# Fourier partial sums through DRAM and a later transposing transfer, in a kernel that weaves attention into an FNet product

## The chip, the cores and the metric

The kernel runs on one core of one Trainium2 chip. The metric is the device time of one execution in microseconds; the core has five engines with a queue each (PE for matrix products, DVE, ACT, POOL, and SP, which here issues every DMA) that are ordered against each other by semaphores alone.

## The reference

Two independent parts, whose results stand side by side in the output (2048 x 1152, f32).

```python
# part A: x [1, 2048, 576], 32 heads of 18, N = 4 segments of L = 512
q, k, v = (x @ wq, x @ wk, x @ wv)          # split in heads and segments
for s in range(4):
    logits = qs @ ks.T * 18 ** -0.5 + mask  # mask: -1e9 where key index > query index
                                            # ar[:, None] < ar[None, :]
    a_dot = softmax(logits) @ vs
    pq = where(qs > 0, qs + 1, exp(qs))
    a_mem = (pq @ M) / (pq @ z + 1e-6)
    o = g * a_mem + (1 - g) * a_dot         # g = sigmoid(beta), per head
    pk = where(ks > 0, ks + 1, exp(ks))
    M += pk.T @ vs ;  z += pk.sum(0)
out_A = o @ wo
# part B: x [1, 2048, 576]
a = x @ dft_hid_re.T ;  b = x @ dft_hid_im.T
out_B = dft_seq_re @ a - dft_seq_im @ b     # dft_seq_*: 2048 x 2048
```

## The kernel before

Products are taken in split precision: a value is written as hi (rounded) plus lo (the rest), and three matmuls (hi lo, hi hi, lo hi) stand for one f32 product. `split` (L53) makes the pair: ACT writes hi, another engine subtracts.

Four stages follow one another.

1. Up to about 234 us: projections of part A, the memory M and its lookup. q, k and v go to DRAM (qd, kd, vd) in three bf16 parts.
2. 234 to 1052 us: attention of part A, woven with all of part B.
3. 1052 to 1060 us: the rest of part B.
4. 1060 to 1132 us: the output product with wo.

Stage 2 is what the change touches. `attention` (L784) is a generator of 68 turns p, each with eight slots. In a turn it advances one even and one odd (segment, head) unit, at several lags at once. An even unit: `s_fill` makes scores on PE into a PSUM tile named s (two buffers) and DVE takes the row minima; `maxima` (POOL) splits these for a group of four heads, `maxima_transpose` turns them on PE (trm), and they go through DRAM (md) into the row block of qs, so that `t_fill` can make transposed scores with the maximum already subtracted; ACT takes the exponential into pf, and hi and lo become phi and plo. An odd unit: `f_fill` makes scores and minima, `f_exp` (ACT) the exponential into pf, `f_split_hi` (ACT) and `f_split_lo` (DVE and POOL) make the pair hl, and `f_turn` issues a transposing DMA from hl into ptt. `pv` then multiplies either kind with the values vst into one PSUM tile, and `pv_out` (DVE) normalises it.

`dense` (L553) is the generator of part B. For ri = 0 (cosine) and ri = 1 (sine) it runs 16 blocks of `hidden` (x times the hidden matrix, results kept in SBUF as AB) and then 16 blocks of `sequence`, each 16 steps of 6 matmuls of 288 columns. In ri = 0 a sequence block is evacuated by ACT into a tile y of its own, 16 of them (128 x 576 f32); in ri = 1 DVE subtracts the second product from that tile and it is stored.

The matrices of part B come in chunks, 160 in all: `chunk(n)` (L506) is called when chunk n is used, issues the load of chunk n + 3 into craw, and splits chunk n + 2 (chi by ACT, clo by POOL). A sequence block uses four chunks, a hidden block one.

The order is written by hand. A loop at L841 takes a slot from `attention`, calls `tick` (which runs what `later` put off by a number of slots, mainly DMA issues), and then takes steps of `dense` until its share of the estimated work, by the numbers in `SLOTS`, catches up:

```python
for w in attention():
    tick()
    ta += w
    while td / total_d < ta / total_a:
        t = next(d, BREAK)
```

So the place of a call in a slot sets how much dense work lies between it and the next. Every engine, SP too, takes its instructions in the order written; SP's queue holds the chunk loads, the twelve row loads and one value load of each group of four heads (`stack_load`), the transposing transfers, md and its readback, and the stores. A tile with `bufs=n` is reused after n allocations, and the instruction that reuses it waits for the last reader.

Of the kernel before, what the change touches and what calls it, by code (L numbers as in the profile page):

```python
# [12 lines left out]
F32 = mybir.dt.float32  # L13
# [23 lines left out]
def infini_attention_and_fnet(ctx: ExitStack, tc: tile.TileContext, xT, wqk, w8, wv, wo, beta, xtT, cT, hT, out):  # L37
# [10 lines left out]
    vd = [dram.tile([P, 4, 8, 220], BF16, name=f"vd{s}") for s in range(NSEG)]  # L48
    amd = [dram.tile([P, D], F32, name=f"amd{t}") for t in range(NT)]
    md = [dram.tile([24, P], BF16, name=f"md{g}") for g in range(32)]  # L50
    od = [dram.tile([8, P, 4, 72], F32, name=f"od{s}") for s in range(NSEG)]

    def split(hi, lo, raw, lo_engine=None):  # L53
# [27 lines left out]
    def later(n, fn, *a):  # L81
        due.setdefault(clock[0] + n, []).append((fn, a))
# [264 lines left out]
    HW, HRAW = {}, {}  # L347

    def h_load(ri, k):
        HRAW[ri, k] = sb.tile([P, D], F32, name="raw", tag="raw", bufs=5 if ri == 0 else 2)  # L350
        dma(HRAW[ri, k], hT[ri, k])

    def h_split(ri, k):
# [8 lines left out]
    def c_load(n):  # L362
        if n < len(CHUNKS) and n not in c_seen:
            c_seen.add(n)
            src, at, k = CHUNKS[n]
            t = sr.tile([P, 5, P], F32, name="craw", bufs=3)
            dma(t[:, :k], src[at])
            c_raw[n] = t

# [32 lines left out]

    NG = 32

    def stack_load(G, lag=21):
        if G >= NG:
            return
        s, g8 = divmod(G, 8)
        rows = slice(g8 * 72, g8 * 72 + 72)
        for buf, src, parts in ((qs_bufs[G % 3], qd[s], QPARTS), (ks_bufs[G % 3], kd[s], KPARTS)):  # L410
            for c, part in enumerate(parts):
                later(1 + c // 2, dma, buf[18 * c:18 * c + 18],
                      src[rows, part, :].rearrange("(h d) t -> d h t", d=DH))

        def values():
            VS[G] = sa.tile([P, 4, 220], BF16, name="vst", bufs=2)
            dma(VS[G], vd[s][:, :, g8])
        later(lag, values)

# [81 lines left out]
            yield 2 * MM  # L501
        yield from edge(True)

    Y, AB = [], []

    def chunk(n):  # L506
        c_load(n + 3)
        c_cut(n + 2)
        return c_split.pop(n)

# [17 lines left out]
        yield BREAK  # L528

    def sequence(ri, tt):  # L530
        if ri == 0:
            Y.append(sb.tile([P, D], F32, name=f"y{tt}"))
        y = Y[tt]

        def evacuate(h, o):
            cs = slice(h * 288, h * 288 + 288)
            if ri == 0:
                act.activation(y[:, cs], o, AF.Copy)
            else:
                dve.tensor_tensor(y[:, cs], y[:, cs], o, OP.subtract)  # L540

        def steps():
            for so in range(NT):
                if so % 4 == 0:
                    hi, lo, _ = chunk(ri * 80 + NT + tt * 4 + so // 4)
                yield hi[:, so % 4], lo[:, so % 4], *AB[ri * NT + so]

        yield from product(steps(), NT, evacuate)
        if ri:
            later(2, dma, out[tt * P:(tt + 1) * P, D:], y)  # L550
        yield BREAK

    def dense():  # L553
        for ri in range(2):
            for tt in range(NT):
                yield from hidden(ri, tt)
            for tt in range(NT):
                late = tt - 8
                if ri == 0 and 0 <= late < 5:
                    h_load(1, late)  # L560
                if ri == 0 and 1 <= late < 6:
                    h_split(1, late - 1)
                if ri and 0 <= late < 5:
                    wo_load(late)
                if ri and 1 <= late < 6:
                    wo_split(late - 1)
                yield from sequence(ri, tt)
# [3 lines left out]
    def o_load(t):  # L571
        if t >= NT:
            return
        s, j = divmod(t, 4)
        a = O3[0].tile([P, D], F32, name="o", bufs=3) if O3 else sb.tile([P, D], F32, name="raw", tag="raw", bufs=2)
        dma(a.rearrange("p (g c) -> p g c", g=8), od[s][:, :, j, :].rearrange("g p c -> p g c"))
        m = None
        if s:
            m = O3[0].tile([P, D], F32, name="oam", bufs=3)
            dma(m, amd[t])  # L580
        O[t] = a, m
# [27 lines left out]
        o_join(t + 1)  # L609

    def wo_load(k):
        raw = sb.tile([P, D], F32, name="raw", tag="raw", bufs=2)
        dma(raw, wo[k])
        WORAW.append(raw)

# [41 lines left out]
    def f_fill(n, kind):  # L657
        o = scores(n, kind)
        if kind == 0:
            F_[n] = [sa.tile([P, 4], F32, name="nb", bufs=2), sa.tile([P, 1280], F32, name="pf", bufs=2), {}]  # L660
        smallest(o, kind, -SCALE, F_[n][0])
        nb = F_[n][0][:, (slice(3, 4), slice(0, 3, 2), slice(1, 2))[kind]]
        dve.tensor_scalar(nb, nb, LIFT, None, op0=OP.add)  # L663
        F_[n][2][kind] = o
# [7 lines left out]

    def f_split_hi(n):
        f = F_[n][1]
        hl = sa.tile([P, 2, 1280], F16, name="hl", bufs=1)
        F_[n][2] = hl
        for a, b in ((512, 1280), (0, 512)):
            act.activation(hl[:, 0, a:b], f[:, a:b], AF.Copy)  # L678
# [5 lines left out]

    def f_turn(n):
        hl = F_.pop(n)[2]
        PT[n] = sa.tile([P, 20, P], F16, name="ptt", bufs=1)
        nc.sync.dma_start_transpose(PT[n], hl.rearrange("p a c -> p (a c)"))  # L688

    def maxima(G):  # L690
        m, b = NEGM[G % 2], MB[G % 2][:, :24].rearrange("p (c n) -> p c n", c=3)
        r = sa.tile([P, 8], F32, name="negx", bufs=2)
        pool.tensor_copy(b[:, 0], m)
        pool.tensor_tensor(r, m, b[:, 0], OP.subtract)
        pool.tensor_copy(b[:, 1], r)
        pool.tensor_tensor(b[:, 2], r, b[:, 1], OP.subtract)
        later(3, maxima_transpose, G)

    def maxima_transpose(G):
        t = ps.tile([P, P], BF16, name="trm", tag="t")  # L700
# [6 lines left out]
    def t_fill(n, kind):  # L707
        G, h = divmod(n, 4)
        q, k = qs_bufs[G % 3][:NPAIR + 3, h], ks_bufs[G % 3][:NPAIR + 3, h]
        if kind == 0:  # L710
            PT[n] = (sa.tile([P, 1280], F16, name="phi", bufs=2), sa.tile([P, 1280], F16, name="plo", bufs=2),
                     sa.tile([P, 1280], F32, name="pf", bufs=2))
        hi, lo, f = PT[n]
        o = ps.tile([P, L], F32, name="t")
        if kind == 0:
            for j in range(4):
                b = slice(j * P, (j + 1) * P)
                pe.matmul(o[:, b], k[:, b], q[:, b], start=True, stop=True)  # L718
            r, w = 0, 512
        elif kind == 1:  # L720
            pe.matmul(o[:, :384], k[:, :128], q[:, 128:], start=True, stop=True)
            r, w = 512, 384
        else:
            pe.matmul(o[:, 256:384], k[:, 256:384], q[:, 384:], start=True, stop=True)
            pe.matmul(o[:, :256], k[:, 128:256], q[:, 256:], start=True, stop=True)  # L725
            r, w = 896, 384
        if kind:
            act.activation(hi[:, r:r + w], o[:, :w], AF.Exp, bias=LIFT, scale=SCALE)  # L728
        act.activation(f[:, r:r + w], o[:, :w], AF.Exp, bias=LIFT, scale=SCALE)  # L729
        if kind == 0:  # L730
            v = f[:, :512].rearrange("p (j q) -> p j q", j=4)
            pool.affine_select(v, v, pattern=[[0, 4], [1, P]], base=0, channel_multiplier=-1,  # L732
                               compare_op=OP.is_ge, fill=0.0)
# [28 lines left out]
    def pv_out(n2):  # L762
# [12 lines left out]
        dve.tensor_tensor(OG[G][:, :, 2 * hh:2 * hh + 2, :].rearrange("p i h d -> p h i d"),  # L775
                          a.rearrange("p (h i) d -> p h i d", h=2), w.to_broadcast([P, 2, 4, DH]), OP.mult)
        if hh == 1:
            later(2, dma, od[s][g8], OG.pop(G).rearrange("p i h d -> p i (h d)"))

    F_LAG, T_LAG, V_LAG = 2, 3, 4  # L780
    NP = 2 * NG
    SLOTS = (560.0, 550.0, 900.0, 1160.0, 890.0, 1060.0, 1210.0, 1160.0)

    def attention():  # L784
        for p in range(NP + V_LAG):
            def even(lag, fn, *a):
                if 0 <= p - lag < NP:
                    fn(2 * (p - lag), *a)
# [9 lines left out]
                o_load(1)  # L798
            if p % 2:
                stack_load(p // 2 + 1)  # L800
            even(V_LAG, pv)
            even(0, s_fill, 0)
            odd(F_LAG + 1, f_exp, 2)
            odd(F_LAG + 1, f_split_hi)
            yield SLOTS[0]
            odd(V_LAG, pv)
            even(T_LAG, t_fill, 0)
            odd(F_LAG + 1, f_split_lo)
            yield SLOTS[1]
            even(0, s_fill, 1)  # L810
            even(T_LAG, t_fill, 1)
            if p >= V_LAG:
                pv_out(p - V_LAG)
            yield SLOTS[2]
            even(0, s_fill, 2)
            yield SLOTS[3]
            odd(F_LAG, f_fill, 0)
            even(T_LAG, t_fill, 2)
            even(T_LAG, t_lo, 1)
            odd(F_LAG + 1, f_turn)  # L820
            if p % 2 and p < NP:
                maxima(p // 2)
            yield SLOTS[4]
            odd(F_LAG, f_fill, 1)
            even(T_LAG, t_hi)
            even(T_LAG, t_lo, 2)
            yield SLOTS[5]
            odd(F_LAG, f_exp, 0)
            even(T_LAG, t_lo, 0)
            yield SLOTS[6]  # L830
            odd(F_LAG, f_exp, 1)
            odd(F_LAG, f_fill, 2)
            yield SLOTS[7]

    d = dense()
# [75 lines left out]
```

## Time and profile before

| | before |
|---|---|
| runs shown, us | 1136.92 median, 1133.63 to 1143.39 (3 runs) |
| profiled execution, us | 1133.77 |
| its span, us | 1132.0 |
| mean granted PE clock | 0.979 |
| PE busy | 1046.5 us, 92% |
| weight loads (PEld) | 958.1 us, 85% |
| DVE busy | 732.0 us, 65% |
| ACT busy | 697.0 us, 62% |
| POOL busy | 607.6 us, 54% |
| DMA, all queues | 185.00 MB, mean 163 GB/s |
| chain that ended last | PE 44%, DMA 14%, DVE 12%, POOL 12%, ACT 8%, issue 7%, SP's queue 3% |

The span runs from the first to the last instruction; the device time holds some 2 us more. A busy time is the union of an engine's instructions; matmuls overlap, so a full PE is not PE at its peak, and its idle time is what lies between busy stretches. A wait is charged to what ended it. The chain is followed back from the last instruction, at each step to what released it. The clock is the share of PE's full rate that was granted.

### The profile page before, as it was taken

Reading aid. Unit: us, or ns where it says so; the run is one execution under the profiler, and the core shown is the slowest. Engines: PE = TensorE matmul, PEld = TensorE weight load, DVE = VectorE, ACT = ScalarE, POOL = GpSimd, SP = SyncE. Lnnn points to the kernel's source line nnn. Section 1 sums busy time; section 2 is a strip of 40 time slices with the busy share of each in tenths; the row PEclk is TensorE's granted clock in tenths of the full one; section 3 lists DMA queues with packets and bytes.
Section 4 is the critical chain, followed back from the end, with each engine's and each line's share of the span. In section 5 each row is a group of like instructions: output and inputs, shape, how many; then the busy total and the mean of one; then the engine's idle time right before and its main releaser. Section 6 shows DMA issues by size and latency. Waiting matters only on the chain.

```text
span 1132.0 us, 25729 instructions
## 1 busy us (share of the span) xinstructions
PE 1046.5 (92%) x9464; PEld 958.1 (85%) x9464; DVE 732.0 (65%) x2095; ACT 697.0 (62%) x1474; POOL 607.6 (54%) x655
## 2 busy tenths in 40 slices
PE   9999999999999799899799899989988898789998
PEld 7889898899988788788788788878878888688998
DVE  6545555746777557668667677767676677675343
ACT  6766565646776557577567677656655566466233
POOL 2465666656666556566556655656555565456100
PEclk9999999999999989999999999989999999989999
DMA  7425253564667756777675766668776779845474
GB/s 247 155 82 183 82 197 120 199 195 123 163 172 171 171 142 148 177 167 183 165 164 133 176 172 158 155 144 189 188 159 169 173 190 183 195 120 139 135 216 140
DMA packets 283133, 185.00 MB, mean 163 GB/s; under 512 B 209984, under 2 KB 242304, under 8 KB 283008
## 3 DMA queue, kind: packets, MB, share of 16 engines
q1 hardware_dynamic: 283008, 183.37, 63.0%
q8 instruction: 74, 1.21, 0.4%
q14 instruction: 51, 0.42, 0.1%
HBM read 102.12 MB, written 39.26 MB: 125 GB/s over the span
## 4 chain that ended last, share of the span: by engine, by line
PE 44%; DMA 14%; DVE 12%; POOL 12%; ACT 8%; issue 7%; SPq 3%; POOLq 0%; DVEq 0%; ACTq 0%
PE d L479 14%; DMA craw<-cT 7%; PE d L77 5%; POOL clo L55 5%; PE v L77 4%; DMA ptt<-hl 3%; PE s L642 3%; DVE s L648 3%; POOL hl L683 2%; PE pv L759 2%; SPq L688 2%; PE d L520 2%; PE d L521 2%; PE d L522 2%; PE qk L224 1%
## 5 line engine op out<-in xcount | busy, mean ns | idle before, releaser
L55 POOL TENSOR_TENSOR clo<-craw,chi 128x512 fp32r<-128x512 f32 x158 | 210.4, 1331 | 212.0 <-ACT chi L54 187.0
L648 DVE CUSTOM_DVE_ANT_0 s<-s,causal 128x512 f32<-128x512 f32 (+3 forms) x512 | 251.7, 497 | 105.9 <-PE s L642 100.7
L479 PE MATMUL d<-wide,chi 128*128 128x288 f32 x1408 | 270.4, 310 | 0.4 <-DVE y L540 0.3
L479 PEld LDWEIGHTS d<-wide,chi 128*128 128x128 f32 x1408 | 216.5, 194 | 13.9 <-issue 11.4
L642 PE MATMUL s<-ks,qs 108*128 108x512 bf16 (+3 forms) x512 | 138.2, 311 | 53.1 <-ACT pf L671 31.1
L479 PE MATMUL d<-wide,clo 128*128 128x288 f32 x704 | 181.7, 325 | 0.0
L54 ACT ACTIVATE chi<-craw 128x512 fp32r<-128x512 f32 x160 | 101.0, 631 | 113.8 <-DMA craw<-cT 98.2
L671 ACT ACTIVATE pf<-s,nb 128x512 f32<-128x512 f32 (+3 forms) x256 | 125.7, 523 | 43.6 <-DVE nb L663 41.0
L479 PEld LDWEIGHTS d<-wide,clo 128*128 128x128 f32 x704 | 120.7, 196 | 17.6 <-issue 15.7
L479 PE MATMUL d<-ab,chi 128*128 128x288 f32 x640 | 128.9, 311 | 0.0
L729 ACT ACTIVATE pf<-t 128x384 f32<-128x384 f32 (+1 forms) x192 | 99.9, 520 | 12.1 <-PE t L718 11.9
L683 POOL TENSOR_TENSOR hl<-pf,hl 128x768 f16<-128x768 f32 x64 | 106.4, 1663 | 0.0
L732 POOL TENSOR_SCALAR_AFFINE_SELECT pf<-pf 128x512 f32<-128x512 f32 x64 | 43.8, 684 | 112.1 <-ACT pf L729 92.6
L683 DVE TENSOR_TENSOR hl<-pf,hl 128x512 f16<-128x512 f32 x64 | 45.9, 717 | 87.5 <-ACT hl L678 33.1
L479 PEld LDWEIGHTS d<-ab,chi 128*128 128x128 f32 x640 | 100.6, 195 | 2.0 <-issue 1.3
L678 ACT ACTIVATE hl<-pf 128x768 f16<-128x768 f32 (+1 forms) x128 | 87.3, 729 | 20.4 <-DMA ptt<-hl 19.0
L728 ACT ACTIVATE phi<-t 128x384 f16<-128x384 f32 x128 | 62.5, 488 | 56.0 <-PE t L725 48.9
L742 DVE TENSOR_TENSOR plo<-pf,phi 128x384 f16<-128x384 f32 (+1 forms) x128 | 95.8, 748 | 0.8 <-ACT phi L737 0.8
L479 PE MATMUL d<-ab,clo 128*128 128x288 f32 x320 | 85.2, 316 | 0.0
L520 PE MATMUL d<-wide,chi 128*128 128x288 f32 x256 | 82.4, 322 | 0.0
L521 PE MATMUL d<-wide,chi 128*128 128x288 f32 x256 | 75.6, 295 | 0.0
L522 PE MATMUL d<-wide,clo 128*128 128x288 f32 x256 | 75.5, 295 | 0.0
(197 smaller groups left out, 2556.3 us busy)
## 6 DMA issues: line engine op xcount, KB each, us to landing
craw<-cT SPq DMA_DIRECT2D x128, 256.0 KB
qs<-qd SPq DMA_DIRECT2D x192, 72.0 KB
ks<-kd SPq DMA_DIRECT2D x192, 72.0 KB
craw<-xtT SPq DMA_DIRECT2D x32, 320.0 KB
out<-y SPq DMA_DIRECT2D x31, 288.0 KB
vd<-vs SPq DMA_DIRECT2D x16, 440.0 KB
vst<-vd SPq DMA_DIRECT2D x32, 220.0 KB
qd<-p SPq DMA_DIRECT2D x16, 384.0 KB
```

What stands on the lines that cost most here:

```text
L54: act.activation(hi, raw, AF.Copy)
L55: (lo_engine or dve).tensor_tensor(lo, raw, hi.bitcast(F32), OP.subtract)
L77: pe.matmul(o, a, b, start=n == 0, stop=n == len(terms) - 1)
L479: pe.matmul(o[h], a, b[:, h * 288:h * 288 + 288], start=start, stop=stop)
L520: pe.matmul(o, xh[:, k], wl[k][:, cs], start=k == 0, stop=False)
L521: pe.matmul(o, xh[:, k], wh[k][:, cs], start=False, stop=False)
L522: pe.matmul(o, xl[:, k], wh[k][:, cs], start=False, stop=False)
L642: pe.matmul(o[:, c:c + w], q[:, i * P:w], k[:, :w], start=True, stop=True)
L648: dve.tensor_tensor_reduce(o[:, c:c + w], o[:, c:c + w], CAUSAL[0][:, L - w:], scale=scale, scalar=-LOWEST, op0=OP.add, op1=OP.min, accum_ ...
L671: act.activation(f[:, FIRST_COL[i]:FIRST_COL[i] + w], o[:, c:c + w], AF.Exp, bias=nb[:, i:i + 1], scale=-1.0)
L683: engine.tensor_tensor(hl[:, 1, a:b], f[:, a:b], hl[:, 0, a:b], OP.subtract)
L729: act.activation(f[:, r:r + w], o[:, :w], AF.Exp, bias=LIFT, scale=SCALE)
```

## The change

The 16 y tiles of the cosine pass are no longer kept in SBUF until the sine pass. A y tile now has four buffers; in the cosine pass it is stored to DRAM tiles yd, in the sine pass each is loaded back one block ahead (`y_load`) and then stored to the output as before. The tiles raw (in the sine pass and for o and wo), phi, plo, pf and vst go from 2 to 3 buffers, craw from 3 to 4, hl and ptt from 1 to 2, and chunk loads are issued one chunk earlier. `f_turn` moves from slot 4 to slot 7, the even `pv` from slot 0 to 3, the odd one from slot 1 to 5, `pv_out` from slot 2 to 6; two of the `t_lo` calls move by one slot. The weights in SLOTS follow the products (560 to 1060, 550 to 1050, 1160 to 660, 1060 to 550; their sum goes from 7490 to 7480). The value loads, the transposing of the maxima and the stores of og are put off by two more slots.

```diff
+    yd = [dram.tile([P, D], F32, name=f"yd{t}") for t in range(NT)]
...
     def h_load(ri, k):
-        HRAW[ri, k] = sb.tile([P, D], F32, name="raw", tag="raw", bufs=5 if ri == 0 else 2)
+        HRAW[ri, k] = sb.tile([P, D], F32, name="raw", tag="raw", bufs=5 if ri == 0 else 3)
...
     def c_load(n):
-            t = sr.tile([P, 5, P], F32, name="craw", bufs=3)
+            t = sr.tile([P, 5, P], F32, name="craw", bufs=4)
...
-    def stack_load(G, lag=21):
+    def stack_load(G, lag=23):
-            VS[G] = sa.tile([P, 4, 220], BF16, name="vst", bufs=2)
+            VS[G] = sa.tile([P, 4, 220], BF16, name="vst", bufs=3)
...
-    Y, AB = [], []
+    Y, AB = {}, []
+
+    def y_load(tt):
+        if tt < NT:
+            Y[tt] = sb.tile([P, D], F32, name="y", bufs=4)
+            dma(Y[tt], yd[tt])
 
     def chunk(n):
-        c_load(n + 3)
+        c_load(n + 4)
         c_cut(n + 2)
...
     def sequence(ri, tt):
-        if ri == 0:
-            Y.append(sb.tile([P, D], F32, name=f"y{tt}"))
-        y = Y[tt]
+        if ri:
+            y_load(tt + 1)
+            y = Y.pop(tt)
+        else:
+            y = sb.tile([P, D], F32, name="y", bufs=4)
...
-        if ri:
-            later(2, dma, out[tt * P:(tt + 1) * P, D:], y)
+        later(2, dma, out[tt * P:(tt + 1) * P, D:] if ri else yd[tt], y)
...
     def dense():
                 yield from hidden(ri, tt)
+            if ri:
+                y_load(0)
...
     def f_fill(n, kind):
-            F_[n] = [sa.tile([P, 4], F32, name="nb", bufs=2), sa.tile([P, 1280], F32, name="pf", bufs=2), {}]
+            F_[n] = [sa.tile([P, 4], F32, name="nb", bufs=2), sa.tile([P, 1280], F32, name="pf", bufs=3), {}]
...
-        hl = sa.tile([P, 2, 1280], F16, name="hl", bufs=1)
+        hl = sa.tile([P, 2, 1280], F16, name="hl", bufs=2)
...
-        PT[n] = sa.tile([P, 20, P], F16, name="ptt", bufs=1)
+        PT[n] = sa.tile([P, 20, P], F16, name="ptt", bufs=2)
...
     def maxima(G):
-        later(3, maxima_transpose, G)
+        later(5, maxima_transpose, G)
...
     def pv_out(n2):
-            later(2, dma, od[s][g8], OG.pop(G).rearrange("p i h d -> p i (h d)"))
+            later(4, dma, od[s][g8], OG.pop(G).rearrange("p i h d -> p i (h d)"))
 
-    SLOTS = (560.0, 550.0, 900.0, 1160.0, 890.0, 1060.0, 1210.0, 1160.0)
+    SLOTS = (1060.0, 1050.0, 900.0, 660.0, 890.0, 550.0, 1210.0, 1160.0)
...
-            even(V_LAG, pv)
             even(0, s_fill, 0)
             odd(F_LAG + 1, f_exp, 2)
             odd(F_LAG + 1, f_split_hi)
             yield SLOTS[0]
-            odd(V_LAG, pv)
             even(T_LAG, t_fill, 0)
             odd(F_LAG + 1, f_split_lo)
             yield SLOTS[1]
             even(0, s_fill, 1)
             even(T_LAG, t_fill, 1)
-            if p >= V_LAG:
-                pv_out(p - V_LAG)
             yield SLOTS[2]
             even(0, s_fill, 2)
+            even(V_LAG, pv)
+            even(T_LAG, t_lo, 1)
             yield SLOTS[3]
             odd(F_LAG, f_fill, 0)
             even(T_LAG, t_fill, 2)
-            even(T_LAG, t_lo, 1)
-            odd(F_LAG + 1, f_turn)
             if p % 2 and p < NP:
                 maxima(p // 2)
             yield SLOTS[4]
             odd(F_LAG, f_fill, 1)
+            odd(V_LAG, pv)
             even(T_LAG, t_hi)
             even(T_LAG, t_lo, 2)
             yield SLOTS[5]
             odd(F_LAG, f_exp, 0)
-            even(T_LAG, t_lo, 0)
+            if p >= V_LAG:
+                pv_out(p - V_LAG)
             yield SLOTS[6]
             odd(F_LAG, f_exp, 1)
             odd(F_LAG, f_fill, 2)
+            even(T_LAG, t_lo, 0)
+            odd(F_LAG + 1, f_turn)
             yield SLOTS[7]
```

More of the change, by code (lines that the diff above doesn't have):

```diff
@@ L574, in o_load @@
         s, j = divmod(t, 4)
-        a = O3[0].tile([P, D], F32, name="o", bufs=3) if O3 else sb.tile([P, D], F32, name="raw", tag="raw", bufs=2)
+        a = O3[0].tile([P, D], F32, name="o", bufs=3) if O3 else sb.tile([P, D], F32, name="raw", tag="raw", bufs=3)
         dma(a.rearrange("p (g c) -> p g c", g=8), od[s][:, :, j, :].rearrange("g p c -> p g c"))
@@ L611, in wo_load @@
     def wo_load(k):
-        raw = sb.tile([P, D], F32, name="raw", tag="raw", bufs=2)
+        raw = sb.tile([P, D], F32, name="raw", tag="raw", bufs=3)
         dma(raw, wo[k])
@@ L710, in t_fill @@
         if kind == 0:
-            PT[n] = (sa.tile([P, 1280], F16, name="phi", bufs=2), sa.tile([P, 1280], F16, name="plo", bufs=2),
-                     sa.tile([P, 1280], F32, name="pf", bufs=2))
+            PT[n] = (sa.tile([P, 1280], F16, name="phi", bufs=3), sa.tile([P, 1280], F16, name="plo", bufs=3),
+                     sa.tile([P, 1280], F32, name="pf", bufs=3))
         hi, lo, f = PT[n]
```

## The prediction

> **What bounds the kernel now.** I read the table of windows first, with its borders where the Fourier passes change: a hidden pass (234 to 308 us and 642 to 726 us) and a sequence pass (308 to 642 and 726 to 1052), each for the cosine and then the sine matrices, all four woven with attention. Columns: the window, its length, then busy time and instructions of PE, weight load, DVE, ACT and POOL, the granted clock, the DMA engines' share, GB/s.
>
> ```profile
> 234.00:308.00 74.00, 72.74 (x643) 68.04 (x643) 48.02 (x157) 47.16 (x112) 45.12 (x56) 1.00 0.59 155
> 308.00:642.00 334.00, 300.57 (x3069) 272.67 (x3068) 228.31 (x728) 216.14 (x450) 193.73 (x205) 0.97 0.70 165
> 642.00:726.00 84.00, 80.41 (x814) 74.19 (x811) 63.67 (x200) 62.05 (x145) 52.67 (x62) 1.00 0.63 154
> 726.00:1052.00 326.00, 289.99 (x2942) 263.24 (x2941) 225.04 (x694) 195.16 (x393) 181.27 (x189) 0.96 0.72 169
> ```
>
> PE is the fullest engine everywhere, so the bound is PE plus its holes. Window less busy time: 1.3 us idle in the first hidden pass (1.7%), 3.6 in the second (4.3%), but 33.4 (10%) and 36.0 (11%) in the sequence passes, 69.4 together. In those the clock is short as well: 0.03 x 334 + 0.04 x 326 = 23 us of clock lost. The attention work is the same in all four; what differs is how fast matrix chunks are eaten. Outside these passes (234 us before, 80 us after) the change does next to nothing.
>
> The waits say who ends the holes (engine and line waited for: us in total, times, longest):
>
> ```profile
> ACT chi L54 <- DMA craw<-cT: 98.2, 44, 7.0
> PE s L642 <- ACT pf L671: 31.1, 24, 4.6
> PE s L642 <- DVE negm L648: 21.4, 27, 3.2
> ACT hl L678 <- DMA ptt<-hl: 19.0, 19, 3.2
> PE pv L759 <- DMA ptt<-hl: 6.8, 9, 1.8
> PE pv L760 <- DVE plo L742: 6.7, 9, 1.7
> PE trm L701 <- POOL mb L696: 6.2, 10, 1.9
> ```
>
> PE mostly waits for a score buffer (s, 52.5 us) that ACT or DVE has not emptied; ACT has not, because it stands before the split of a chunk that has not landed. One turn of this, from the chain of waits (start, us, what) and the SP queue's and ACT's timelines (start, duration):
>
> ```profile
> 735.56 1.62 POOL hl L683
> ...
> 741.50 3.89 DMA craw<-cT
> ...
> 746.17 1.28 POOL clo L55
> ...
> 749.98 0.59 PE s L642
> ```
>
> ```profile
> 737.21 3.61 SPq L688 DMA_TRANSPOSE ptt<-hl  x1
> 740.87 0.59 SPq L417 DMA_DIRECT2D vst<-vd  x1
> 741.50 0.62 SPq L367 DMA_DIRECT2D craw<-cT  x1
> ```
>
> ```profile
> 745.47 0.63 ACT L54 ACTIVATE chi<-craw 128x512 fp32r<-128x512 f32 x1 [4.86 <-DMA craw<-cT]
> ```
>
> SP is one queue. It stands at the transposing transfer until POOL ends hl (735.56 + 1.62 = 737.18, issue at 737.21), spends 3.6 us issuing it, and only then comes to the chunk; ACT idles 4.86 us, with the exponentials that free the score buffers queued behind.
>
> **The change, part by part.** No compute instruction is added or removed; 16 stores and 16 loads of 288 KB are.
>
> *Chunk loads, one more buffer, issued one chunk earlier (c_load(n+4)).* The reused buffer is read at the same chunk as before, so no new wait arises. For all chunks but the first I took from the trace the time from a load's issue to the end of ACT's instruction before that chunk's split: median 5.4 us, a tenth under 0.6. The loads that ACT waited for landed 3.8 us after issue in the median, 5.3 at the ninth decile. The same time from the issue of the load one place earlier: never under 5.0, median 10.0, a twentieth under 6.7. So nearly every one of the late chunks would have been there. How much of PE's wait that is: I followed each s wait over 0.3 us back through the trace; those through a late chunk are 40 of 61 us counted start to start, two thirds. 52.5 x 0.65 = 34 us. Bounds: 0, if ACT and DVE run into something else at once, and 52.5.
>
> *Transposing transfers at slot 7 instead of 4, hl and ptt doubled, products later.* A weight unit of 1000 in SLOTS is 1.6 us now (818 us / 68 turns / 7.49). POOL's hl stands in slot 1; the transfer had 2610 units (4.2 us) after it and gets 5260 (8.4), so SP stops waiting for POOL there (it idles 100 us before such issues in the trace) and the chunk loads, score rows and maxima placed in slots 4 to 6 no longer queue behind it. Behind it now stand the next turn's chunk loads and, every second turn, stack loads. From transfer to product it was 4880 units, 7.8 us, and is 5720, 9.2; landing took 6.0 us after issue in the median where PE waited. plo of the first quarter to its product: 2370 units (3.8 us) become 4170 (6.7). The transposed maxima wait five ticks, not three: 1950 units (3.1 us) become 3810 (6.1). The three waits of 6.8, 6.7 and 6.2 us have longest members of 1.8, 1.7 and 1.9, less than, or about, what is added. I take 15 of 19.7; bounds 0 and 19.7. ACT's 19.0 on ptt goes with the second hl; it is part of the s waits and not counted again. The price: score rows from qs<-md are loaded 3980 units (6.4 us) ahead of their product instead of 6040 (9.7). In the trace they were issued 11.6 us ahead in the median and 6.8 at least; 3.3 less leaves 8.3 and 3.5, against the 2.9 us (median) that the md write before them took to land. Costed at 0, the next thing to be late.
>
> *Clock.* Half-rate stretches follow the holes:
>
> ```profile
> 393.00:396.40 3.40, 0.43 (x18) 0.35 (x14) 0.00 (x0) 0.00 (x0) 0.00 (x0) 1.00 0.80 220
> 396.40:403.20 6.80, 5.17 (x40) 4.62 (x40) 1.80 (x4) 3.72 (x8) 2.41 (x3) 0.52 0.13 45
> 837.40:840.10 2.70, 0.94 (x22) 0.83 (x18) 0.07 (x1) 1.72 (x4) 1.18 (x1) 1.00 0.98 208
> 840.10:843.50 3.40, 3.40 (x36) 2.98 (x35) 1.39 (x3) 1.96 (x3) 1.03 (x3) 0.55 0.88 289
> ```
>
> The clock is 0.52 after 3 us without PE work and 0.55 after 1.8. If 34 + 15 of 69.4 us of holes go, I let the 23 us fall in proportion: 16 us. Bounds 0 and 23.
>
> The Trainium skill (TensorE: Matmul & The Clock Gate, section Part 1: The HAM clock gate) says that the array falls to half rate after an idle window of about 3.4 us. The stretch after the 1.8 us hole says that part of a window is enough here. Read strictly, the rule would charge only the three holes of over 3.3 us, each followed by 6.8 us at half rate, 10 us in all; this term would then be 10 and the sum 6 smaller.
>
> *Partial sums through DRAM.* In the first sequence pass each y is stored two ticks after its evacuation; in the second it is loaded a whole block ahead (96 products of 132 ns, 12.7 us, and the attention between). 32 issues at about 0.4 us are 13 us of SP's queue over 660 us; SP stands 200 us ahead of transposes, md readbacks and og stores in the trace, time that such issues can use. 9.4 MB against 165 GB/s at a share of 0.70 (236 GB/s when full) is 40 us of the 16 engines, their share going to about 0.77. A store waits for ACT's evacuation, with chunk loads queued behind it; out<-y waits for DVE now at the same place, 13.9 us in 5 times (longest 8.3). Their cover is the second chunk of lead. I take 0; without that cover each would make a chunk late by its landing, 32 x 3.9 = 125 us of ACT's waiting, and ACT's waiting costs PE about 50/105 of itself (50 us of holes and clock to 105 us on chunks): +59. Below nothing is excluded: it only adds work.
>
> *The rest* (buffers of raw, vst, phi, plo, pf; value loads two ticks later; even products and pv_out in later slots, weights moved with them) changes order, not amount; pv_out leaves the slot of two score reductions for one with none. 0, bounds -6 to +6: the s waits that pass through pv_out are about 6 us.
>
> Sum: 34 + 15 + 16 = 65 us. The profiled execution took 1133.8 us (span 1132.0 and 1.8 around it), near the low end of the runs shown, 1133.6 to 1143.4, median 1136.9. 1133.8 - 65 = 1069, and 1072 from the median; I say **1069**. The windows check it: sequence passes at the second hidden pass's idle share (4.3% of 660 = 28) and full clock would gain 41 + 23 = 64.
>
> **Rivals.**
> *PE closes up* to the first hidden pass's 1.7%: 69.4 - 11.2 + 23 = 81, more from the last hidden pass: 1050 or less. For it: the same attention ran that tight once. Against: no sequence pass, with a chunk every 5 us, did. 0.20.
> *The wait moves.* ACT waits 41 us on DVE's nb (L663), DVE 101 on PE's s: with chunks on time the score loop itself, two buffers, holds PE. Then half the chunk term and the 15 stay, the clock hardly moves: 17 + 15 = 32, 1102. For it: a third of the s waits never touched a chunk. 0.25.
> *No effect*: SP's queue, still one, stands as often, now at transfers before the next chunk; chunks come as late, gains of 5 to 10 are cancelled: 1125 to 1143. Against: the 5.0 us minimum above. 0.05.
> *Slower*: the stores hold SP until ACT has evacuated and take the DMA engines, so that a chunk is late at each of the 32; extra lead is eaten, chunk gain and clock 0. 1133.8 + 59 - 15 = 1178. It decides once a load is issued less than its 3.9 us landing ahead of the split. Against: 13.9 us in all is what y stores cost SP today. 0.08.
>
> **How the numbers follow.** Forecast 0.42 (1050 to 1090), the rivals as given. Runs differ by 0.9%, so 1% is about what can be told. Faster: 0.42 + 0.20 + 0.25 = 0.87; within: 0.05; slower: 0.08. The range runs from 1035, where all 69 + 23 us of holes and clock (1042) and some of the hidden passes' 5 and of the edges are gone, to 1122, the wait-moves case with 20 us of its gain lost.
>
> **What would show it.** ACT's wait on craw<-cT falls from 98 to under 20 us; PE's s waits from 52 to about 18; the waits on ptt, plo and mb nearly vanish; clock 0.99 in the sequence passes; PE over 95% busy there; POOL's clo waits less for chi; y loads ended before DVE's y. Wrong if ACT still waits 50 us or more on craw, if waits on y<-yd, qs<-md or pv appear on PE or DVE, or if s waits stay with craw gone.

## The result and the profile after

The changed kernel takes 1068.47 us (median of 4 runs, 1067.08 to 1068.80) against 1135.28 us before (4 runs); the ratio is 0.940, interval 0.935 to 0.945. The profiled execution took 1068.6 us, its span 1066.9 us, at a mean clock of 0.99.

The windows of the changed kernel, again with borders where the Fourier passes change (columns as above):

```profile
235.00:307.00 72.00, 72.00 (x611) 67.98 (x610) 49.72 (x151) 46.76 (x113) 44.24 (x55) 1.00 0.64 163
307.00:611.00 304.00, 293.17 (x3089) 268.56 (x3088) 241.91 (x734) 217.36 (x451) 192.13 (x206) 0.99 0.87 194
611.00:690.00 79.00, 78.80 (x804) 73.49 (x803) 69.71 (x196) 59.16 (x142) 52.75 (x62) 1.00 0.90 180
690.00:990.00 300.00, 286.04 (x2979) 263.60 (x2979) 235.62 (x694) 195.77 (x396) 180.18 (x189) 0.98 0.89 197
```

PE idles 10.8 and 14.0 us in the sequence passes, 24.8 where it was 69.4, and 0.2 us in the hidden passes where it was 4.9. Clock lost: 0.01 x 304 + 0.02 x 300 = 9 us where it was 23. That is 44.6 + 4.7 + 14 = 63 of the 65 us between the two profiled executions. Two more columns moved: the DMA share of the sequence passes, from 0.70 and 0.72 to 0.87 and 0.89, and DVE's busy time.

PE's longest waits of the changed kernel in stage 2 (us in total, times, longest):

```profile
PE s L651 <- DMA craw<-cT: 6.5, 5, 2.3
PE s L651 <- ACT pf L680: 5.6, 7, 1.9
PE s L651 <- ACT hl L687: 4.0, 2, 2.1
...
PE s L651 <- DVE negm L657: 3.1, 3, 1.4
PE s L651 <- DMA vst<-vd: 2.0, 1, 2.0
```

The waits on ptt, plo and mb (19.7 us) are gone, and ACT no longer waits for a cosine or sine chunk (98.2 us before). What is left on s is 24 us, and its largest kind is new: it ends on a DMA. A score product reads neither craw nor vst; the profile infers these names from semaphores, and here the transfer named can't be the operand. The loads that such a product does need are the score rows of its group of four heads. The longer of these waits stand about 23 us or a multiple of it apart, and a group takes about 23 us; the runs below treat them as waits for rows.

### The profile page after: what moved, and what is told of

Read it like the earlier page. It is cut to its first block, busy times and chain, and to the rows that moved or that the text cites. A ratio compares the mean times of both kernels' runs of the same rounds, so it can differ in the third digit from the quotient of the medians.

```text
span 1066.9 us, 25805 instructions
## 1 busy us (share of the span) xinstructions
PE 1031.3 (97%) x9464; PEld 952.7 (89%) x9464; DVE 764.1 (72%) x2095; ACT 695.3 (65%) x1474; POOL 602.8 (57%) x655
## 4 chain that ended last, share of the span: by engine, by line
PE 78%; ACT 7%; DVE 6%; DMA 4%; issue 3%; POOL 2%; SPq 0%; DVEq 0%; POOLq 0%; ACTq 0%
PE d L480 33%; PE s L651 6%; PE d L78 6%; PE v L78 4%; PE d L526 3%; PE pv L768 3%; PE d L527 3%; PE d L528 3%; PE qk L225 2%; DMA craw<-cT 2%; PE pv L769 2%; PE qk L78 1%; DVE r L241 1%; PE look L329 1%; PE t L727 1%
## 5 line engine op out<-in xcount | busy, mean ns | idle before, releaser
L56 POOL TENSOR_TENSOR clo<-craw,chi 128x512 fp32r<-128x512 f32 x158 | 217.9, 1380 | 153.6 <-ACT chi L55 122.1
L480 PEld LDWEIGHTS d<-wide,chi 128*128 128x128 f32 x1408 | 212.2, 191 | 4.6 <-issue 3.7
L480 PE MATMUL d<-wide,clo 128*128 128x288 f32 x704 | 175.9, 317 | 0.0
L751 DVE TENSOR_TENSOR plo<-pf,phi 128x384 f16<-128x384 f32 (+1 forms) x128 | 125.6, 981 | 2.3 <-ACT pf L738 2.3
L480 PE MATMUL d<-ab,chi 128*128 128x288 f32 x640 | 126.2, 307 | 0.0
L480 PEld LDWEIGHTS d<-wide,clo 128*128 128x128 f32 x704 | 117.4, 192 | 1.5
L651 PEld LDWEIGHTS <-qs 108*128 108x128 bf16 x512 | 40.0, 98 | 46.1 <-issue 13.7
L528 PE MATMUL d<-wide,clo 128*128 128x288 f32 x256 | 75.5, 295 | 0.0
```

The source lines that it names most:

```text
L56: (lo_engine or dve).tensor_tensor(lo, raw, hi.bitcast(F32), OP.subtract)
L480: pe.matmul(o[h], a, b[:, h * 288:h * 288 + 288], start=start, stop=stop)
L528: pe.matmul(o, xl[:, k], wh[k][:, cs], start=False, stop=False)
L651: pe.matmul(o[:, c:c + w], q[:, i * P:w], k[:, :w], start=True, stop=True)
L751: (pool if kind == 2 else dve).tensor_tensor(lo[:, a:b], f[:, a:b], hi[:, a:b], OP.subtract)
```

## The experiments

Ratios are to the kernel before, run beside each; its median was 1138 to 1140 us there. The changed kernel's own ratio, 0.940, is the one above.

**E1: the partial sums alone.** Of the change only `yd`, `y_load` and the four-buffer `y`; nothing else.

> The kernel before with the partial sums alone kept in DRAM (16 stores, 16 loads of 288 KB; y has 4 buffers), every other buffer and the order as before. Lead theory and queue theory both say that the transfers are hidden: 1136 us, ratio to before 0.99 to 1.01. Rival (the stores hold SP's queue and chunks come later): ACT's wait on chunks grows from 98 us to 140 or more, time 1150 us or more, ratio over 1.012.

1149.2 us, ratio 1.009 (1.006 to 1.012), a loss of about 10 us. The result lies between the forecasts: the ratio is just inside the band of the first (0.99 to 1.01), the time is 1 us short of the rival's 1150, and ACT's wait on chunks grew, but not to 140. Its waits, ACT's and then PE's:

```profile
ACT chi L55 <- DMA craw<-cT: 114.0, 44, 8.2
...
PE s L651 <- ACT pf L680: 35.2, 24, 5.2
PE pv L768 <- DMA ptt<-hl: 11.1, 12, 2.8
```

The same waits as before, and most of them some microseconds longer: the transfers are not hidden. From the profiled execution before to this one both sequence passes grew by 7 us, that with the stores and that with the loads; these two executions lie 15 us apart, the medians 9, so part of the 7 is the spread of the runs.

**E2: E1 and the chunks' lead.**

```diff
-            t = sr.tile([P, 5, P], F32, name="craw", bufs=3)
+            t = sr.tile([P, 5, P], F32, name="craw", bufs=4)
...
-        c_load(n + 3)
+        c_load(n + 4)
```

> E1 plus the fourth craw buffer with chunk loads issued one chunk earlier; the attention's order and its other buffers as before. Lead theory (34 us of holes and two thirds of the clock's 16): ACT's wait on chunks falls from 98 to under 20 us, time about 1091 us, ratio 0.96. Queue theory (SP standing at the transposing transfer is what counts, and the loads behind it stay late whatever their lead): ACT still waits 50 us or more on chunks, time 1115 us or more, ratio over 0.98.

1101.8 us, ratio 0.967 (0.963 to 0.970), 4% below E1. ACT's chunk wait is 1.4 us, as the lead theory has it, but the time lies 11 us over its forecast. PE's and ACT's waits say where that went:

```profile
ACT hl L687 <- DMA ptt<-hl: 58.0, 33, 4.5
...
PE pv L768 <- DMA ptt<-hl: 29.7, 20, 4.0
PE s L651 <- DVE negm L657: 9.0, 10, 2.4
...
PE s L651 <- ACT pf L680: 2.5, 4, 1.1
```

The s waits fell from 57 us in E1 to 12, and the wait for the transposed operand rose from 11 to 30: PE now arrives at the product before the transfer has landed. It gets there 6.0 us after the issue of the transfer in the median (6.5 in E1), and where it waits, the transfer is there 6.4 us after its issue (5.6 in E1).

**E3: the changed kernel without the lead** (the two lines of E2 turned back).

> The changed kernel with three craw buffers and the chunk loads where they were before the change; all else changed. Lead theory: ACT waits 50 us or more on chunks again and the kernel gives back about 45 of the 67 us: 1113 us, ratio to before 0.98. Queue theory: with the transposing transfer at slot 7, SP is free in slots 4 to 6, chunks come in time with three buffers, ACT waits under 25 us on them, time 1080 us or less, ratio 0.95 or less.

1078.7 us, ratio 0.947 (0.944 to 0.951). The time is the queue theory's, ACT's wait on chunks is the lead theory's (50 us or more):

```profile
ACT chi L55 <- DMA craw<-cT: 51.9, 27, 5.9
...
PE s L651 <- ACT pf L680: 19.9, 19, 3.3
```

Half of ACT's chunk wait is there again, yet the time is only 0.8% above the changed kernel's (9 us; the two intervals just meet). So the new order and the other buffers, without the lead, already take 6% off E1. The lead and the order replace each other in large part; the prediction had added them.

**E4: the changed kernel with the attention's old order** (slots, weights and lags of before; every buffer and the lead kept).

> The changed kernel with the attention's old order: transposing transfer in slot 4, products in slots 0 and 1, pv_out in slot 2, the old weights and lags; all buffers and the earlier chunk loads stay changed. Lead theory: E2 and a little for the doubled hl, ptt: 1085 us, ratio 0.955, PE's waits on ptt, plo and mb stay near 20 us. Queue theory: SP stands as before, 1110 us or more, ratio over 0.977.

1092.7 us, ratio 0.959 (0.955 to 0.962). The lead theory's shape: ACT waits 3.5 us on chunks, but PE waits long on ptt, and 3.2 us on plo and 4.4 on mb:

```profile
PE pv L768 <- DMA ptt<-hl: 29.4, 18, 4.2
```

Against the changed kernel the order is worth 2%, about 22 us of time. Against E2 the other buffers are worth 9 us. Doubling hl and ptt does not help PE's wait on ptt (29.7 in E2); ACT's, 58 us there, is gone.

**E5: only the transposing transfer back in slot 4.**

```diff
             even(T_LAG, t_fill, 2)
+            odd(F_LAG + 1, f_turn)
...
             even(T_LAG, t_lo, 0)
-            odd(F_LAG + 1, f_turn)
```

> The changed kernel with the transposing transfer alone back in slot 4; products, pv_out, weights, buffers and chunk loads stay changed. Distance theory (with the chunks' lead in place the order is worth the time between transfer and product, and SP's standing no longer matters): product 8370 units after the transfer, PE's wait on ptt under 2 us, time as the changed kernel within 1%: 1062 to 1080 us, ratio to before 0.935 to 0.95. Queue theory (the later place frees SP for the chunk and row loads): s waits on row loads and chunks come back, SP stands some 80 us at the transfer, time 1085 us or more, ratio over 0.955.

1067.1 us, ratio 0.937 (0.935 to 0.938): the changed kernel's time. The queue theory's loss does not come. SP does stand at the transfer again until POOL has ended hl, 80 us in all (110 in the kernel before, 21 in the changed kernel), but what this costs and what it saves offset each other. PE's s waits fall from 24 to 11 us, and a new wait of 14 us appears:

```profile
PE t L727 <- DMA qs<-md: 13.7, 10, 2.6
...
PE s L651 <- DMA ks<-kd: 3.8, 6, 1.1
```

The readback of the maxima, which the prediction named as next to be late, is late when the transfer stands ahead of it; the score rows, which no longer stand behind the transfer, are in time. So the worth of the order lies in its other parts. The part that bears on ptt is the later product: it starts 6.5 us after the transfer's issue in E4 (median), 10.8 in the changed kernel and 11.9 here, and PE waits on ptt in E4 alone. No run moved the products by themselves.

**E6: the partial sums stored and loaded twice**, in the changed kernel; the second copy is used by nothing.

```diff
+    yd2 = [dram.tile([P, D], F32, name=f"yz{t}") for t in range(NT)]
...
             dma(Y[tt], yd[tt])
+            dma(sb.tile([P, D], F32, name="yx", bufs=1), yd2[tt])
...
         later(2, dma, out[tt * P:(tt + 1) * P, D:] if ri else yd[tt], y)
+        if ri == 0:
+            later(2, dma, yd2[tt], y)
```

> The changed kernel with every partial sum stored twice and loaded twice (the second copy goes into DRAM tiles and an SBUF tile that nothing else uses): 32 more transfers, 9.4 MB more. Cover theory (E1's loss of about 1% came through chunks that had no lead; with the lead it is hidden): 1068 to 1074 us, ratio to before under 0.947. Rival (traffic costs wherever it stands, the engines' share being 0.88 already): another 10 us or more, 1079 us or more, ratio over 0.95.

1088.0 us, ratio 0.955 (0.953 to 0.957): 18 us more for 9.4 MB. The cover theory falls. ACT's chunk wait stays at 2 us or less; what grew are the s waits that end on a DMA, 30 us in all where the changed kernel has 9. The largest kind:

```profile
PE s L655 <- DMA craw<-cT: 13.8, 8, 3.7
```

**E7: the score rows three slots earlier.** E6 pointed at the rows, so here their loads are called in slot 5 of the even turn; the longer lag leaves the value load where it was.

```diff
-    def stack_load(G, lag=23):
+    def stack_load(G, lag=26):
...
-            if p % 2:
-                stack_load(p // 2 + 1)
...
             odd(F_LAG, f_fill, 1)
+            if p % 2 == 0:
+                stack_load(p // 2 + 1)
             odd(V_LAG, pv)
```

> The changed kernel with the loads of a group's score rows issued three slots earlier (from slot 5 of the even turn, ahead of the transposing transfer instead of behind it; the value load keeps its place). Row theory (PE's s waits that end on a DMA, some 8 us, and the clock after them are rows that land late behind the transfer): these waits vanish, 1056 to 1062 us, ratio to the changed kernel 0.99 to 0.994. Rival (the rows push the transfer or the chunks instead): 1068 us or more.

1059.4 us, ratio 0.930 (0.927 to 0.933), about 1% below the changed kernel, as the row theory has it. The s waits on a DMA fell to 0.5 us and all s waits from 24 to 11; 4.8 us of PE on ptt and 10.6 us of ACT on chunks came back.

**E8: E7, and the stores of y four slots later** (`later(6, ...)`).

> E7 with the stores of partial sums and of part B's output put off by four more slots, so that SP does not stand (41 us in the trace) for DVE's y ahead of other loads. Queue theory: another 2 to 5 us, 1052 to 1058 us. Rival (SP has time to stand there, nothing behind it is late): as E7 within 2 us.

1055.0 us, ratio 0.926 (0.923 to 0.929), the lowest of all runs. Its interval overlaps that of E7, so this last step is likely and not settled. In its sequence passes the clock is 1.00, and PE idles 7.8 and 8.3 us:

```profile
307.00:604.00 297.00, 289.23 (x3061) 265.31 (x3057) 238.07 (x730) 213.98 (x445) 191.23 (x205) 1.00 0.86 198
682.00:981.00 299.00, 290.73 (x3086) 267.95 (x3085) 242.12 (x713) 196.78 (x402) 183.49 (x192) 1.00 0.87 202
```

**E9: E8 with the partial sums twice**, as in E6, to see whether the rows were the whole price of the traffic.

> E8 with the partial sums stored and loaded twice, as in E6. Row theory of the traffic's price (E6 lost 18 us because PE's s waited for score rows that landed later beside the added transfers; nothing else was exposed): with the rows three slots earlier the second copy costs under 8 us, 1055 to 1063 us, ratio to before under 0.934. Rival (the engines' share of 0.87 itself is the price, whoever waits): again 15 us or more, 1070 us or more, ratio over 0.939.

1073.1 us, ratio 0.943 (0.939 to 0.947): again 18 us. The row theory of the price falls. The rows are in time now, and other transfers are late instead (ACT's wait on chunks is 16.4 us as well, 10.4 in E8):

```profile
PE pv L772 <- DMA ptt<-hl: 10.8, 11, 3.4
PE s L655 <- ACT pf L684: 9.0, 9, 3.1
```

So the price belongs to the traffic, and it showed in whichever transfer had least slack. Whether it is bytes on the engines or the time of SP's queue stays open: both were doubled together.

**E10: E8 without the lead** (the two lines of E2 turned back).

> E8 with three craw buffers and chunk loads as before the change. If the chunk's lead is worth what E3 showed (about 9 us once the order is changed): 1062 to 1068 us, ratio to before 0.932 to 0.938, ACT waiting 50 us or more on chunks. Rival (rows ahead of the transfer put the chunks further behind, so that without lead they are late again in full): 1080 us or more, ACT waiting 80 us or more.

1119.4 us, ratio 0.983 (0.978 to 0.988). Three buffers instead of four cost 64 us here and 9 us in E3: the rival.

```profile
ACT chi L55 <- DMA craw<-cT: 89.7, 33, 6.5
...
PE s L651 <- ACT pf L680: 52.3, 30, 4.1
```

With the rows ahead of them in the queue the chunk loads need the second chunk of lead.

**E11: E8 with the transposing transfer in slot 5, ahead of the rows.**

> E8 with the transposing transfer in slot 5, ahead of the rows, instead of slot 7. Distance theory (E8's remaining 3 us of PE waits on ptt and 10 us of ACT waits on chunks come from SP reaching the transfer late): ptt waits vanish, rows still come in time, 1050 to 1055 us, within 1% of E8. Rival (the rows behind the transfer are late again, as in the changed kernel): 1062 us or more and s waits on DMA of 5 us or more.

1064.2 us, ratio 0.935 (0.931 to 0.939), 1% above E8: the rival's time, not its waits. PE's waits on ptt did vanish, but 7.0 us on qs<-md came, ACT's on cosine and sine chunks went from 10 to 18 us, and s waits on a DMA are below 2 us. One queue serves all four kinds of load; moving one forward made two others later.

## Why the prediction was right

The forecast was 1069 us and the measurement 1068. By term it was less exact, and that the errors offset each other was luck.

*What bounds the kernel.* Right. Holes and lost clock of the sequence passes made up the gain almost alone (59 of 65 us), and E2 shows the chain: with the chunks in time the s waits fall from 57 to 12 us. Of the signs of being wrong one is there, and slight: DVE waits on PE's pv once, for 6.8 us (once before too, for 3.3).

*Chunk loads, 34 us of holes.* Right in mechanism. ACT's chunk wait went from 98 to 0 (forecast: under 20), the s waits from 52.5 to 24 (forecast: about 18). With its two thirds of the clock the term is 45 us, and the lead was worth 47 on E1 (4%). But the term is no fixed amount: it was 9 us beside the new order (E3) and 64 beside E8's.

*Transposing transfers and later products, 15 us.* The waits went as said, all three to nothing. With its third of the clock the term is 20 us; measured after the lead, the order is worth 22 (E4) and the other buffers, hl and ptt among them, 9 more (E2 against E4). It was undersized, since it was read from a kernel in which late chunks hid the lateness of the transfer: with the lead and the old order PE waits 29.4 us on ptt alone. One reason given for it came true and was no net source of time: SP stops standing for POOL (110 us before, 21 after), but E5 puts 80 us of that standing back and loses nothing.

*Clock, 16 us.* 14 measured. In stage 2 of the changed kernel no PE wait is longer than 2.3 us, and yet five holes of 1.8 to 2.1 us are each followed by 3.4 us at half rate; the second sequence pass still has a clock of 0.98. Two more holes, of 2.0 and 2.3 us, are not followed by one, so the length of a hole alone does not decide. The Trainium skill (TensorE: Matmul & The Clock Gate, Part 1: The HAM clock gate) asks for an idle window of about 3.4 us. The trace decides: shorter holes cost clock here. Of the three holes of over 3.3 us that the prediction counted in the kernel before, two are that long (4.6 and 4.0 us); the third is 3.2.

*Partial sums, 0.* The step that failed. I called them covered by the second chunk of lead. They cost about 10 us alone (E1), and the same traffic once more costs 18 us with the lead (E6) and 18 with the rows in time (E9). With the lead in place the chunks were not what the traffic made late (E6), so the cover named was the wrong one. The share forecast, 0.77, was for the old length of the passes. The same working with the new length gives 0.84, and 0.87 to 0.89 was measured; the rest stays open. That the changed kernel itself pays some 10 to 18 us for its own copy is an inference from these runs and was not measured: with y kept in SBUF (16 tiles of 2304 bytes per partition, 36.9 KB, instead of 9.2) and the new buffers it was not run.

*Next to be late.* I named the readback of the maxima. In the changed kernel it is the score rows, which the text had put behind the transfer without a price; E7 prices them at 1%. The readback is late in E5 and E11.

So the sum of 65 us was met because an undersized term and an uncounted cost offset each other. Step by step, from the kernel before over E1, E2 and E4 to the changed kernel, the runs give -10, 47, 9 and 22 us, 68 in all by these ratios; the prediction had 0, then 45, then 20 for the last two together. In another order of steps the terms are others (E3), though the sum is the same. The rival in which the wait moves is not all wrong either: in E2 the lead alone moves it, though to ptt and not to the score loop.

## What to carry to other kernels

When several transfers share one queue, the slack of each must be priced together: giving one a buffer or an earlier place makes the next one visible, and terms read from waits in the old trace neither add nor stay. Read the waits again after each single step (E1, E2, E4 here), and price "hidden" traffic by doubling it: it costs one run, gives the price of one more copy, and showed here that the traffic was not hidden. An edit that leaves the time alone (E5) need not have left the waits alone: two of them had changed places. Where a product waits for a transfer, try a later product first; moving the transfer alone gained nothing here (E5) and lost 1% in E11, because it makes other loads of the same queue late.

## What the hardware showed that was not expected

DVE's subtract became slower with the new order, same shapes and counts (groups by form, before and then after: busy us, mean ns):

```profile
L742 DVE TENSOR_TENSOR plo<-pf,phi 128x384 f16<-128x384 f32 x64 | 49.3, 770 | 0.0
```

```profile
L751 DVE TENSOR_TENSOR plo<-pf,phi 128x384 f16<-128x384 f32 x64 | 66.0, 1032 | 2.3 <-ACT pf L738 2.3
```

With the 512-column form this is 30 of DVE's 32 us of added busy time. What differs as well is the work of POOL beside it. In the changed kernel's trace the 384-column form takes 0.99 us on average beside POOL's subtract for clo (30 cases), 1.24 beside that for hl (25), and 0.55 to 0.62 beside POOL's other instructions or none (9). Before, 16 of the 64 stood beside clo or hl, 16 beside POOL's own plo (0.91 us), and the other 32 at 0.55 to 0.64. So it is not POOL's being busy as such that goes with the longer time, but which instruction it runs. No engine waits for plo in the changed kernel's trace, and no run took POOL's work away, so the cause is argued only.

Issuing a transposing transfer held SP for 3.1 us in the median before and for 4.0 us after (64 issues each; longest 4.9 and 6.0), with the DMA share of the sequence passes at 0.70 to 0.72 and at 0.87 to 0.89. All 64 together held the queue for 216 us before and 259 after, 43 us more; what lengthens an issue was not tried.
